# An attention and two-MoE kernel on one Trainium2 core: scores of a head pair in two PSUM groups instead of four, masks first, and the first weights' bit operations on every second slot

## The chip, the cores and the metric

The kernel runs on one core of one Trainium2 chip, which computes the whole output. The metric is the device time of the execution in microseconds; 3 runs of the kernel before are shown. A profiled execution of it gives the trace that is read here.

## What is computed

The reference, cut to what matters. Attention over 2 batches of 12 heads (448 positions, 64 wide), then two feed-forward stages on 896 tokens:

```python
scores = where(triu(ones, k=1), -1e9, q @ k.T / 8)      # causal, 24 heads of 448 x 448
p = exp(scores - max(scores)); attn = p / (sum(p) + 1e-9)
x = (attn @ v)                                          # -> 896 x 768
x = (sigmoid(x @ w_gate) * (x @ w_val)) @ w_out         # 768 -> 1536 -> 768
h = x @ w_in                                            # 768 -> 1024
out = (layernorm(h * softmax(h)) * g_ln) @ w_out2       # 1024 -> 768
```

All is held as a high and a low part (`hi`, `lo = value - hi`), and a product is three matmuls: hi·hi, hi·lo, lo·hi.

## The kernel before

The 24 heads are worked as 12 pairs p = 0 to 11. A head has four row blocks i = 0 to 3 of 128 query rows (block 0 has 64 new rows); block i sees keys 0 to QE[i], that is 64, 192, 320, 448 columns. For every block and both heads of a pair: the score matmuls (L333, `s`, six of 64 rows, two heads at a time on the two halves of the array), the mask added by a matmul with an identity (L336), the row maximum on VectorE (DVE, L354), exp with its row sum on ScalarE (ACT, L360, an ACTIVATE and a read of its accumulator for each head). Then sums (L366, GpSimd = POOL), reciprocals (L371, DVE), normalising of the probabilities `p` in place (L379, POOL), transposes on TensorE (PE, L404, `t`, four units a pair: (unit 1, head 0), (1, 1), (0, 0), (0, 1)), their split into hi (`tr_hi`, ACT L411) and lo (`tr_lo`, DVE L225 `pt`), and the product with v (L434, `x`, eight chunks a pair), split by `x_hi` (ACT L218 `xy`) and `x_lo` (DVE L225 `xy`). The splits of k and q for the next pair stand in the same loop: `k_hi` on ACT, `k_lo` on DVE (L225 `qks`), `q_hi` on POOL, `q_lo` on DVE (L245); those of v on POOL (`v_hi` L220, `v_lo` L225).

Nothing is scheduled by a tool: the loop `for s in range(slots + 34)` issues instructions by hand, and every engine works through its own list in the order in which it was issued. A pair has 8 slots. `SIDE`, `UNIT0` and `PV0` say in which slot, counted from the pair's own first, a step is issued; within a slot PE's work comes first, then ACT's, DVE's, POOL's. Waits between engines are put in by the framework from what a tile reads and writes. Two instructions of different engines on the same PSUM bank of one tile are always made to wait for each other, two readers included.

Scores have the pool `ps_s`: two buffers of `[128, 2, 512]` floats, one PSUM bank for each head of the pair. Before, each row block has a buffer of its own, so a pair goes through four, at slots 0, 2, 4, 6, in the order of `ORD` (blocks 3, 2, 1, 0).

From slot 74 on (pair 9's third slot) the loop also carries the bit operations that turn the first weight chunks, read from HBM as 64-bit words, into float32 (`bits_steps`: L112 on ACT, then L115, L117, L120 on DVE, then `dma_next` issues the load of a later chunk on SP), and the split of a chunk (`chunk_hi` ACT L131, `chunk_lo` DVE L134). From slot 96 on PE has `early_tiles`: 36 matmuls (L467, `gv`) of the first gate and value tile for batch 0, two a slot. After the loop follow the gate and value matmuls (L592), 383 us up to the end.

Of the kernel before, what the change touches and what calls it, by code (L numbers as in the profile page):

```python
# [10 lines left out]
F32 = mybir.dt.float32  # L11
# [24 lines left out]
NEG = -1e30  # L36
TERMS = ((0, 0), (0, 1), (1, 0))
# [7 lines left out]
def attn_moe_moe2(ctx: ExitStack, tc: tile.TileContext, qk, v, w_gv, w_out, w_in2, w_out2, g_ln, out):  # L45
# [3 lines left out]
    nc = tc.nc  # L49
# [11 lines left out]
    identb = const.tile([128, 128], BF16, name="identb")  # L61
    maskb = const.tile([128, 128], BF16, name="maskb")
# [111 lines left out]
    NE = 1  # L174
# [15 lines left out]
    with ExitStack() as actx:  # L190
# [4 lines left out]
        st = actx.enter_context(tc.tile_pool(name="st", bufs=2, side="right"))  # L195
        ps_s = actx.enter_context(tc.tile_pool(name="ps_s", bufs=2, space=PSUM, reuse_waits="tile"))
# [3 lines left out]
        NH = B * H  # L200
# [88 lines left out]
        NPB = 6  # L289
# [21 lines left out]

        rs_t, pt_t, ps_sc, ps_tr, ps_pv = {}, {}, {}, {}, {}

        def slot(s):

            return s // 8 * 2 + s % 2, ORD[s % 8 // 2]


        def sc_mm(s):
            if s % 2:  # L320
                return
            both = ps_s.tile([128, 2, 512], F32, tag="s", name="s")
# [17 lines left out]
        def sums_of(s):  # L340
            h, i = slot(s)
            t = sum_t[h // 2 % 3]
            k = NQ * (1 - h % 2) + i
            return t[:, k:k + 1], t[:, 8 + k:9 + k]

        def sc_max(s):
            if s % 2:
                return
            if s == 0:
                for e in range(2):  # L350
                    nc.vector.reduce_max(out=sums_of(e)[1], in_=ps_sc[e], axis=AX.X, negate=True)
                return
            h, i = slot(s)
            nc.vector.reduce_max(out=sum_t[h // 2 % 3][:, 8 + i:16:NQ], in_=ps_sc.pop((s, 2)), axis=AX.X, negate=True)  # L354

        def sc_exp(s):
            h, i = slot(s)
            n = QE[i]
            sm, mx = sums_of(s)
            nc.scalar.activation(out=p_t[h % NPB][:, POFF[i]:POFF[i] + n], in_=ps_sc.pop(s), func=AF.Exp,  # L360
                                 bias=mx, scale=1.0, accum_out=sm)


        def sums(p, u):
            rs = rs_t[p, u] = st.tile([128, 8], F32, tag=f"rs{u}", name="rs")
            nc.gpsimd.tensor_scalar(out=rs[:, 4:8].rearrange("p (a i) -> p a i", a=2),  # L366
                                    in0=sum_t[p % 3][:, 0:8].rearrange("p (a i) -> p a i", a=2)[:, :, 2 - 2 * u:4 - 2 * u],
                                    scalar1=EPS_SUM, scalar2=0.0, op0=ALU.add, op1=ALU.add)

        def recips(p, u):  # L370
            nc.vector.reciprocal(out=rs_t[p, u][:, 0:4], in_=rs_t[p, u][:, 4:8])  # L371

        def normalise(p, u):
            r = rs_t.pop((p, u))
            for i in (3 - 2 * u, 2 - 2 * u):
# [45 lines left out]
        def pv_mm(pr):  # L421
            ps = ps_pv[pr] = ps_x.tile([128, S], F32, tag="x", name="x")
            terms = {(a, j): iter(TERMS) for a in range(2) for j in range(NQ)}
            n = 0
            for chunk in CHUNKS:
                for w in chunk.split():
                    sec, j = int(w[0]), int(w[1])
                    h = 2 * pr + sec
                    u = 1 if j in UNITS[1] else 0
                    c0 = {0: 0, 1: 0, 2: 320, 3: S}[j]  # L430
                    a, c = next(terms[sec, j])

                    l = v3[pr % 2][:, a] if j == 3 else v2[pr % 2][:, a, j, (1 - sec) * D:(3 - sec) * D]
                    nc.tensor.matmul(out=ps[:, 128 * j:], lhsT=l, rhs=pt_t[h][:, c, u, c0:c0 + S - 128 * j],  # L434
                                     start=(n == 0), stop=(n == 20),
                                     skip_group_check=True)
                    n += 1
                yield
# [16 lines left out]
        def early_tiles():  # L455
# [23 lines left out]
        UNIT0 = {(1, 0): 11, (1, 1): 13, (0, 0): 15, (0, 1): 17}
        PV0 = 15  # L480

        SIDE = dict(
            kh=-6, qh=-6, kl=-4, ql=-3, sm0=5, rc0=6, nm0=6, lk=7, sm1=9, rc1=10, nm1=10, vh=12, vl=13, xh=23, xl=24)
        STEP = dict(
            qh=(prep_q_hi, 'P'), kh=(prep_k_hi, 'A'), kl=(prep_k_lo, 'D'), ql=(prep_q_lo, 'D'),
            vh=(prep_v_hi, 'P'), vl=(prep_v_lo, 'P'), lk=(last_keys, 'P'), xh=(x_hi, 'A'), xl=(x_lo, 'D'),
        )
        for u in range(2):
            STEP[f"sm{u}"] = (lambda p, u=u: sums(p, u)), 'P'
            STEP[f"rc{u}"] = (lambda p, u=u: recips(p, u)), 'D'  # L490
            STEP[f"nm{u}"] = (lambda p, u=u: normalise(p, u)), 'P'

        def side(s, eng):
            for name, s0 in SIDE.items():
                p, e = divmod(s - s0, 8)
                first = 1 if name[0] in "qk" else 0
                if STEP[name][1] == eng and e == 0 and first <= p < NH // 2:
                    STEP[name][0](p)
# [12 lines left out]
        for s in range(slots + 34):

            if (s - PV0) % 8 == 0 and 0 <= (s - PV0) // 8 < NH // 2:
                pv_now = pv_mm((s - PV0) // 8)
            at(sc_mm, s)
            if s in (2, 4, 6):
                keep_warm(24 if s == 2 else 8)
            for _ in range(2):  # L520
# [3 lines left out]
            next(pv_now, None)

            if s % 2 == 0:
                at(sc_exp, s - 2)
                at(sc_exp, s - 1)
            units(tr_hi, s - 1)
            side(s, 'A')  # L530

            side(s, 'D')
            units(tr_lo, s - 2)
            at(sc_max, s)

            side(s, 'P')
            side(s, 'S')
# [243 lines left out]
```

## Time and profile before

| | us |
|---|---|
| median of 3 runs (516.86 to 518.14) | 517.78 |
| the profiled execution | 517.47 |
| its span, from the first to the last instruction | 515.6 |
| PE busy / DVE / ACT / POOL | 501.2 (97%) / 335.7 / 227.0 / 141.9 |
| granted TensorE clock, mean | 0.992 |
| HBM traffic | 101 GB/s over the span |

Times in the rows below are microseconds from the span's start, "mean ns of one" apart. In a timeline a row is: start, duration, engine, line, operation, output <- inputs, shape, count, and in brackets the idle time of the engine just before it and what ended it. Matmuls overlap: a row of PE reaches into the next one. The granted clock is a share of 2.4 GHz: 1.00 is the full level, 0.50 the lower one, 1.2 GHz.

### The profile page before, as it was taken

The numbers are of one execution on the slowest core, as the hardware profiler recorded it, in microseconds if no ns is written. First come the engines' busy times: TensorE is split into PE (matmuls) and PEld (weight loads), VectorE is DVE, ScalarE is ACT, GpSimd is POOL, SyncE is SP. The second block draws the span as 40 slices with busy tenths as digits, with TensorE's granted clock in tenths as the row PEclk, the third lists the DMA queues.
The fourth block names the chain that finished last, engine by engine and source line by source line (L and its number), as shares of the span: only waits on it lengthen the run. The fifth ranks groups of instructions, "written<-read, shape, count | busy, mean of one in ns | idle before, by whom it ended". The sixth has DMA issues, their size and how long they took to land.

```text
span 515.6 us, 7727 instructions
## 1 busy us (share of the span) xinstructions
PE 501.2 (97%) x2900; PEld 448.9 (87%) x2900; DVE 335.7 (65%) x532; ACT 227.0 (44%) x481; POOL 141.9 (28%) x275
## 2 busy tenths in 40 slices
PE   8799999888999999999999999999999999999997
PEld 7588887778899999999999999999998888899997
DVE  6688878896356678877777766666763878741210
ACT  5677878673424443454345432432323243332211
POOL 2998888683000000000000000000051487720000
PEclk9999999799999999999999999999999999999999
DMA  5723232221122354444334531443450231000101
GB/s 149 214 67 105 64 107 58 82 83 62 62 89 96 103 161 128 160 163 141 122 112 158 184 107 59 163 163 123 163 182 2 72 114 62 0 32 31 62 32 61
DMA packets 13205, 52.80 MB, mean 102 GB/s; under 512 B 1776, under 2 KB 2288, under 8 KB 13168
## 3 DMA queue, kind: packets, MB, share of 16 engines
q1 hardware_dynamic: 13168, 52.31, 30.7%
q8 instruction: 23, 0.38, 0.3%
q14 instruction: 14, 0.11, 0.1%
HBM read 49.55 MB, written 2.75 MB: 101 GB/s over the span
## 4 chain that ended last, share of the span: by engine, by line
PE 90%; POOL 5%; DVE 2%; ACT 1%; issue 1%; POOLq 0%; ACTq 0%
PE gv L592 33%; PE pm L622 17%; PE po L713 11%; PE h L652 11%; PE x L434 5%; PE s L333 4%; PE t L404 4%; POOL p L379 3%; PE s L336 1%; PE gv L467 1%; PE tp L695 1%; PE warm L304 1%; ACT p L360 1%; POOL v L225 1%; POOL rs L366 0%
## 5 line engine op out<-in xcount | busy, mean ns | idle before, releaser
L592 PE MATMUL gv<-xy,hl 128*128 128x448 f32 x828 | 168.1, 365 | 0.6 <-ACT pre L472 0.6
L592 PEld LDWEIGHTS gv<-xy,hl 128*128 128x128 f32 x828 | 155.4, 188 | 13.3 <-ACT pre L472 1.0
L622 PE MATMUL pm<-g,hl 128*128 128x448 f32 x432 | 87.7, 365 | 0.0
L622 PEld LDWEIGHTS pm<-g,hl 128*128 128x128 f32 x432 | 81.1, 188 | 6.4
L639 POOL TENSOR_SCALAR t<-t,g_sb 128x768 f32<-128x768 f32 x8 | 9.0, 1121 | 257.9 <-PE pm L622 257.9
L134 DVE TENSOR_TENSOR hl<-t,hl 128x768 fp32r<-128x768 f32 x36 | 34.6, 962 | 40.9 <-ACT hl L131 39.2
L713 PE MATMUL po<-wo,lt 128*128 128x384 f32 x336 | 60.7, 340 | 0.0
L652 PE MATMUL h<-wi,xy 128*128 128x512 f32 x252 | 59.2, 395 | 0.0
L434 PE MATMUL x<-pt,v 128*128 128x320 f32 (+3 forms) x252 | 59.2, 336 | 0.0
L713 PEld LDWEIGHTS po<-wo,lt 128*128 128x128 f32 x336 | 58.7, 188 | 0.2 <-POOL wo L644 0.2
L652 PEld LDWEIGHTS h<-wi,xy 128*128 128x128 f32 x252 | 47.2, 187 | 11.4
L360 ACT ACTIVATE p<-s,sum 128x448 f32<-128x448 f32 (+3 forms) x96 | 44.9, 476 | 25.0 <-DVE sum L354 18.6
L117 DVE SCALAR_TENSOR_TENSOR t<-raw,t 128x768 int32<-128x768 int32 (+1 forms) x56 | 53.7, 958 | 1.8
L112 ACT ACTIVATE raw<-raw 128x768 f32<-128x768 f32 (+1 forms) x56 | 48.2, 868 | 12.2 <-DMA raw<-in_wo_dram 7.9
L120 DVE SCALAR_TENSOR_TENSOR t<-raw,t 128x768 int32<-128x768 int32 (+1 forms) x56 | 51.1, 913 | 1.6
L379 POOL TENSOR_SCALAR p<-p,rs 128x448 f32<-128x448 f32 (+3 forms) x96 | 47.1, 509 | 7.2 <-DVE rs L371 6.7
L354 DVE TENSOR_REDUCE sum<-s 128x2 f32<-128x640 f32 (+3 forms) x47 | 31.8, 677 | 15.5 <-PE s L336 15.3
L434 PEld LDWEIGHTS x<-pt,v 128*128 128x128 f32 x252 | 40.0, 195 | 0.4
L225 DVE TENSOR_TENSOR pt<-t,pt 128x512 fp32r<-128x512 f32 (+1 forms) x48 | 32.1, 668 | 5.1 <-ACT pt L411 4.8
L115 DVE TENSOR_SCALAR t<-raw 128x768 int32<-128x768 int32 (+1 forms) x56 | 30.7, 548 | 5.3 <-ACT raw L112 5.2
L333 PE MATMUL s<-qks 64*128 64x448 f32 (+3 forms) x288 | 32.9, 334 | 0.7 <-ACT p L360 0.7
L171 DVE TENSOR_TENSOR lt<-tp,lt 128x512 fp32r<-128x512 f32 x14 | 9.7, 690 | 36.4 <-ACT lt L170 36.4
(84 smaller groups left out, 518.7 us busy)
## 6 DMA issues: line engine op xcount, KB each, us to landing
raw<-in_gv_dram SPq DMA_DIRECT2D x24, 768.0 KB, 4.4
raw<-in_wo_dram SPq DMA_DIRECT2D x20, 768.0 KB, 4.4
raw<-in_wi_dram SPq DMA_DIRECT2D x12, 512.0 KB, 3.5
qkr<-in_qk_dram SPq DMA_DIRECT2D x22, 224.0 KB, 3.7
vr<-in_v_dram SPq DMA_DIRECT2D x12, 256.0 KB, 3.7
out_dram<-o SPq DMA_DIRECT2D x6, 384.0 KB, 2.3
qkr<-in_qk_dram SPq DMA_DIRECT2D x4, 112.0 KB, 2.7
out_dram<-o SPq DMA_DIRECT2D x2, 192.0 KB, 1.9
```

What stands on the lines that cost most here:

```text
L112: nc.scalar.activation(out=w1.bitcast(F32), in_=w1.bitcast(F32), func=AF.Copy, scale=2.0 ** -112)
L117: nc.vector.scalar_tensor_tensor(out=tt, in0=w1, scalar=-2 ** 31, in1=tt, op0=ALU.bitwise_and, op1=ALU.bitwise_or)
L120: nc.vector.scalar_tensor_tensor(out=tt, in0=w0, scalar=29, in1=tt, op0=ALU.logical_shift_right, op1=ALU.bitwise_or)
L225: (nc.gpsimd if eng == 'P' else nc.vector).tensor_tensor(out=out, in0=a, in1=b, op=ALU.subtract)
L333: nc.tensor.matmul(out=ps[e], lhsT=flat[rows, cq * S + n - 128:cq * S + n], rhs=t[rows, ck, :n], start=(m == 0), stop=False)
L360: nc.scalar.activation(out=p_t[h % NPB][:, POFF[i]:POFF[i] + n], in_=ps_sc.pop(s), func=AF.Exp, bias=mx, scale=1.0, accum_out=sm)
L379: nc.gpsimd.tensor_scalar(out=t, in0=t, scalar1=r[:, k:k + 1], scalar2=1.0, op0=ALU.mult, op1=ALU.mult)
L434: nc.tensor.matmul(out=ps[:, 128 * j:], lhsT=l, rhs=pt_t[h][:, c, u, c0:c0 + S - 128 * j], start=(n == 0), stop=(n == 20), skip_group_chec ...
L592: nc.tensor.matmul(out=ps[i, b], lhsT=w[:, a, cs], rhs=xy[kk][:, x, b * S:(b + 1) * S], start=(kk == 0 and a == 0 and x == 0), stop=(kk == ...
L622: nc.tensor.matmul(out=ps[b], lhsT=w[:, a, cs], rhs=g_t[kk][:, x, b * S:(b + 1) * S], start=(kk == 0 and a == 0 and x == 0), stop=(kk == N ...
L652: nc.tensor.matmul(out=h[:, n * 512:(n + 1) * 512], lhsT=xy[kk][:, a, tk], rhs=wi[n * NK + kk][:, c], start=(kk == 0 and i == 0), stop=(kk ...
L713: nc.tensor.matmul(out=ps[n], lhsT=lts[k // 4][:, a, k % 4], rhs=wo[k][:, c, cs], start=(k == 0 and i == 0), stop=(k == NF2 - 1 and i == 2))
```

## The change

1. **Two groups a pair.** `GROUPS = [(3, 0), (2, 1)]`: blocks 3 and 0 share one bank per head (448 + 64 = 512 columns), and blocks 2 and 1 (320 + 192 = 512). A pair takes two buffers of `ps_s`, at slots 0 and 4. Within a group the four masks come first (the first of each bank opens it), then the twelve score matmuls.
2. **The steps of a pair** stand in one list `STEPS`: maxima at slots 0, 1, 4, 5, exps at 1, 2, 5, 6; the sums move from POOL to DVE, ahead of the reciprocals (slots 3 and 7); normalising at slots 4 (blocks 3, 0) and 8 (blocks 2, 1) on POOL, where before it was at 6 (blocks 3, 2) and 10 (blocks 1, 0). For pair 0 the second head is normalised on DVE. Splits of k, q and v move by one to three slots, `x_lo` from 24 to 23. Transposes and v products keep their slots.
3. **The first weights' bit operations** start at slot 88 in place of 74, a step every second slot, nine slots a chunk in place of ten.
4. `keep_warm` (matmuls without use at the start) three times 24, at slots 2, 5, 9, in place of 24, 8, 8 at 2, 4, 6.

```diff
+GROUPS = [(3, 0), (2, 1)]
-ORD = [3, 2, 1, 0]
...
-        def sc_mm(s):
-            if s % 2:
-                return
+        def sc_mm(p, g):
             both = ps_s.tile([128, 2, 512], F32, tag="s", name="s")
...
+            for i in GROUPS[g]:
+                n = QE[i]
+                w = min(n, 128)
+                ps = ps_sc[p, i] = both[:, :, c0:c0 + n]
+                for e in range(2):
+                    nc.tensor.matmul(out=ps[:, e, n - w:], lhsT=identb, rhs=maskb[:, 128 - w:],
+                                     start=(c0 == 0), stop=False, skip_group_check=True)
+                c0 += n
+            for i in GROUPS[g]:
+                n = QE[i]
+                for m, (cq, ck) in enumerate(((1, 0), (1, 3), (2, 0))):
...
-        def sums(p, u):
-            rs = rs_t[p, u] = st.tile([128, 8], F32, tag=f"rs{u}", name="rs")
-            nc.gpsimd.tensor_scalar(out=rs[:, 4:8].rearrange("p (a i) -> p a i", a=2),
...
+        def recips(p, g):
+            rs = rs_t[p, g] = st.tile([128, 8], F32, tag=f"rs{g}", name="rs")
+            i = slice(0, 4, 3) if g == 0 else slice(1, 3)
+            nc.vector.tensor_scalar(out=rs[:, 4:8].rearrange("p (a i) -> p a i", a=2),
+                                    in0=sum_t[p % 3][:, 0:8].rearrange("p (a i) -> p a i", a=2)[:, :, i],
+                                    scalar1=EPS_SUM, scalar2=None, op0=ALU.add)
+            nc.vector.reciprocal(out=rs[:, 0:4], in_=rs[:, 4:8])
...
+                    eng = nc.vector if p == 0 and a else nc.gpsimd
...
+            (1, 'A', lambda p: sc_exp(p, 3)), (2, 'A', lambda p: sc_exp(p, 0)),
+            (5, 'A', lambda p: sc_exp(p, 2)), (6, 'A', lambda p: sc_exp(p, 1)),
+            (0, 'D', lambda p: sc_max(p, 3)), (1, 'D', lambda p: sc_max(p, 0)),
+            (4, 'D', lambda p: sc_max(p, 2)), (5, 'D', lambda p: sc_max(p, 1)),
...
-            if s in (2, 4, 6):
-                keep_warm(24 if s == 2 else 8)
+            if s in (2, 5, 9):
+                keep_warm(24)
...
-                e = s - 74 - 10 * c
+                e = s - 88 - 9 * c
                 if e == 0:
                     bits_now = bits_steps(c)
-                if 0 <= e < 4:
+                if e in (0, 2, 4, 6):
                     next(bits_now)
-                if e == 5 and c < 2 * NE:
+                if e == 7 and c < 2 * NE:
                     chunk_hi(c)
-                if e == 6 and c < 2 * NE:
+                if e == 8 and c < 2 * NE:
                     chunk_lo(c)
```

Three places show what moved. First, DVE in a middle pair, from one pair's widest maximum on, with the semaphores that an instruction waits for (`Activation_49` is counted up by ACT, `PE_49` by PE). Before (L354 the maxima, L371 the reciprocals):

```order
L354 TENSOR_REDUCE sum_141<-s 128x2 [waits PE_49]
L225 TENSOR_TENSOR pt<-t,pt 128x448 [waits Activation_49]
L371 RECIPROCAL rs<-rs 128x4 [waits Pool_49]
L354 TENSOR_REDUCE sum_141<-s 128x2 [waits PE_49]
L225 TENSOR_TENSOR pt<-t,pt 128x512 [waits Activation_49]
L225 TENSOR_TENSOR qks<-qkr,qks 128x448 [waits DMAHW4_49,DMAHW5_49,DVE_49,Activation_49]
L354 TENSOR_REDUCE sum_141<-s 128x2 [waits PE_49]
L245 SCALAR_TENSOR_TENSOR qks<-qkr,qks 128x448 [waits Pool_49]
L225 TENSOR_TENSOR pt<-t,pt 128x512 [waits DVE_49,Activation_49]
L371 RECIPROCAL rs<-rs 128x4 [waits Pool_49]
L354 TENSOR_REDUCE sum_141<-s 128x2 [waits PE_49]
```

After (L347 the maxima, L361 the sums, L364 the reciprocals), from the widest maximum to the fourth and what follows it:

```order
L347 TENSOR_REDUCE sum_139<-s 128x2 [waits PE_49]
L225 TENSOR_TENSOR pt<-t,pt 128x448 [waits Activation_49]
L347 TENSOR_REDUCE sum_139<-s 128x2 [waits Activation_49]
L225 TENSOR_TENSOR qks<-qkr,qks 128x448 [waits DMAHW1_49,DMAHW0_49]
L225 TENSOR_TENSOR pt<-t,pt 128x512 [waits Activation_49]
L361 TENSOR_SCALAR rs<-sum_139 128x4 [waits Activation_49]
L364 RECIPROCAL rs<-rs 128x4 [waits DVE_49]
L347 TENSOR_REDUCE sum_139<-s 128x2 [waits PE_49]
L225 TENSOR_TENSOR pt<-t,pt 128x512 [waits Activation_49]
L347 TENSOR_REDUCE sum_139<-s 128x2 [waits Activation_49]
L245 SCALAR_TENSOR_TENSOR qks<-qkr,qks 128x448 [waits Pool_49]
L225 TENSOR_TENSOR pt<-t,pt 128x512 [waits Activation_49]
```

Before, each of the four maxima waits for PE alone; now the first of a group waits for PE and the second for ACT, which has just read the other columns of the same bank.

Second, PE in a middle pair. Before, the two smaller blocks (L333 scores, L336 masks, L404 transposes, L434 v products):

```order
L333 MATMUL s<-qks 128x192 x6
L336 LDWEIGHTS identb
L336 MATMUL s<-maskb,identb 128x128
L336 LDWEIGHTS identb
L336 MATMUL s<-maskb,identb 128x128
L434 MATMUL x<-pt,v_1_136 128x448
L404 MATMUL t<-identx,p_145 128x128
L404 MATMUL t<-ident,p_145 128x128 x4
L434 MATMUL x<-pt,v_1_136 128x448 x2
L333 MATMUL s<-qks 128x64 x6
```

After, the second group of a pair (L334 scores, L325 masks, L429 v products):

```order
L325 LDWEIGHTS identb
L325 MATMUL s<-maskb,identb 128x128
L325 LDWEIGHTS identb
L325 MATMUL s<-maskb,identb 128x128
L325 LDWEIGHTS identb
L325 MATMUL s<-maskb,identb 128x128
L325 LDWEIGHTS identb
L325 MATMUL s<-maskb,identb 128x128
L334 MATMUL s<-qks 128x320 x6
L334 MATMUL s<-qks 128x192 x6
L429 MATMUL x<-pt,v_1_136 128x448
```

The six matmuls of a small block now follow those of a large one with no transposes or v products between.

Third, DVE where the first weight chunk's bit operations begin. Before, in pair 9, three slots in a row:

```order
L354 TENSOR_REDUCE sum_139<-s 128x2
L225 TENSOR_TENSOR pt<-t,pt 128x512
L115 TENSOR_SCALAR t<-raw 128x768
L225 TENSOR_TENSOR qks<-qkr,qks 128x448
L354 TENSOR_REDUCE sum_139<-s 128x2
L117 SCALAR_TENSOR_TENSOR t<-raw,t 128x768
L245 SCALAR_TENSOR_TENSOR qks<-qkr,qks 128x448
L225 TENSOR_TENSOR pt<-t,pt 128x512
L120 SCALAR_TENSOR_TENSOR t<-raw,t 128x768
```

After, in pair 11, which has no k and q of a next pair to split:

```order
L347 TENSOR_REDUCE sum_141<-s 128x2
L115 TENSOR_SCALAR t<-raw 128x768
L225 TENSOR_TENSOR pt<-t,pt 128x512
L361 TENSOR_SCALAR rs<-sum_141 128x4
L364 RECIPROCAL rs<-rs 128x4
L347 TENSOR_REDUCE sum_141<-s 128x2
L117 SCALAR_TENSOR_TENSOR t<-raw,t 128x768
L225 TENSOR_TENSOR pt<-t,pt 128x512
L347 TENSOR_REDUCE sum_141<-s 128x2
L120 SCALAR_TENSOR_TENSOR t<-raw,t 128x768
```

The three operations stand where the splits of k and q stood in the pairs before, or beside a maximum that waits.

## Rows read from the trace of the kernel before

**Rows 1.** Busy time by stretch: length, then each engine's, clock, DMA share, GB/s

```profile
30.31:81.57 51.26, 51.26 (x433) 41.70 (x432) 42.92 (x79) 40.28 (x134) 44.73 (x97) 1.00 0.32 85
81.57:132.53 50.96, 45.12 (x316) 37.95 (x315) 38.25 (x61) 30.15 (x85) 30.64 (x61) 0.93 0.25 81
132.53:515.60 383.07, 379.74 (x1904) 348.70 (x1904) 234.56 (x332) 137.22 (x203) 47.40 (x73) 1.00 0.30 103
```

**Rows 2.** Timeline of PE, pair 5: its widest block, and what follows

```profile
47.40 0.89 PE L333 MATMUL s<-qks 64*128 64x448 f32 x6
...
48.31 0.60 PE L434 MATMUL x<-pt,v 128*128 128x320 f32 x3
```

**Rows 3.** Timeline of PE around the bit operations: starts of pairs 9 and 11, waits

```profile
81.57 0.89 PE L333 MATMUL s<-qks 64*128 64x448 f32 x6
...
91.75 0.45 PE L404 MATMUL t<-identx,p 128*128 128x128 f32 x1 [2.43 <-DVE pt L225]
...
104.26 0.88 PE L333 MATMUL s<-qks 64*128 64x448 f32 x6
...
118.73 0.33 PE L404 MATMUL t<-identx,p 128*128 128x128 f32 x1 [1.12 <-POOL p L379]
...
132.53 0.69 PE L592 MATMUL gv<-xy,hl 128*128 128x448 f32 x2 [0.62 <-ACT pre L472]
```

**Rows 4.** Timelines of DVE and POOL there, and the stretch of lower clock

```profile
88.50 1.71 DVE L117 SCALAR_TENSOR_TENSOR t<-raw,t 128x768 int32<-128x768 int32 x1
...
91.52 0.94 DVE L120 SCALAR_TENSOR_TENSOR t<-raw,t 128x768 int32<-128x768 int32 x1
...
88.39 2.12 POOL L225 TENSOR_TENSOR v<-vr,v 128x384 fp32r<-128x384 f32 x2
...
91.70:97.80 6.10, 6.05 (x28) 5.05 (x28) 4.65 (x9) 3.16 (x11) 3.30 (x7) 0.50 0.48 167
```

**Rows 5.** Timeline of DVE, pair 5

```profile
48.54 1.09 DVE L354 TENSOR_REDUCE sum<-s 128x2 f32<-128x896 f32 x1 [0.72 <-PE s L336]
...
50.73 0.83 DVE L354 TENSOR_REDUCE sum<-s 128x2 f32<-128x640 f32 x1 [0.48 <-PE s L336]
...
52.18 0.79 DVE L225 TENSOR_TENSOR qks<-qkr,qks 128x448 fp32r<-128x448 f32 x1
52.89 0.55 DVE L354 TENSOR_REDUCE sum<-s 128x2 f32<-128x384 f32 x1
53.36 0.61 DVE L245 SCALAR_TENSOR_TENSOR qks<-qkr,qks 128x448 fp32r<-128x448 f32 x1
53.89 0.68 DVE L225 TENSOR_TENSOR pt<-t,pt 128x512 fp32r<-128x512 f32 x1
...
54.64 0.29 DVE L354 TENSOR_REDUCE sum<-s 128x2 f32<-128x128 f32 x1
...
55.75 0.62 DVE L225 TENSOR_TENSOR xy<-x,xy 128x448 fp32r<-128x448 f32 x1
```

**Rows 6.** Timeline of ACT, pair 5: first and last instruction of two blocks' exps

```profile
49.73 0.64 ACT L360 ACTIVATE p<-s,sum 128x448 f32<-128x448 f32 x1 [1.54 <-DVE sum L354]
...
50.87 0.20 ACT L360 ACTIVATION_READ_ACCUMULATOR p<-s,sum 128x1 f32 x1
...
51.90 0.54 ACT L360 ACTIVATE p<-s,sum 128x320 f32<-128x320 f32 x1
...
52.82 0.22 ACT L360 ACTIVATION_READ_ACCUMULATOR p<-s,sum 128x1 f32 x1
```

**Rows 7.** Timeline of DVE: widest maxima of pairs 0 and 2, last reciprocals of pair 11

```profile
7.88 1.16 DVE L351 TENSOR_REDUCE sum<-s 128x1 f32<-128x448 f32 x2 [1.44 <-PE s L336]
...
22.47 1.09 DVE L354 TENSOR_REDUCE sum<-s 128x2 f32<-128x896 f32 x1 [1.21 <-PE s L336]
...
117.98 0.17 DVE L371 RECIPROCAL rs<-rs 128x4 f32<-128x4 f32 x1
```

**Rows 8.** Costliest groups, the page's section 5: normalising on POOL

```profile
L379 POOL TENSOR_SCALAR p<-p,rs 128x448 f32<-128x448 f32 (+3 forms) x96 | 47.1, 509 | 7.2 <-DVE rs L371 6.7
```

More of the change, by code (lines that the diff above doesn't have):

```diff
@@ L340, in sums_of @@
[L340 to L354, printed above, removed]
@@ L370, in recips @@
[L370 to L375, printed above, removed]
+        def sc_mm(p, g):
+            both = ps_s.tile([128, 2, 512], F32, tag="s", name="s")
+            t = qk_sp[p]
+            flat = t.rearrange("p c s -> p (c s)")
+            c0 = 0
+            for i in GROUPS[g]:
[9 more added lines that the diff above has]
+                for m, (cq, ck) in enumerate(((1, 0), (1, 3), (2, 0))):
+                    for e in range(2):
+                        rows = slice(e * D, (e + 1) * D)
+                        nc.tensor.matmul(out=ps_sc[p, i][:, 1 - e], lhsT=flat[rows, cq * S + n - 128:cq * S + n],
+                                         rhs=t[rows, ck, :n], start=False, stop=(m == 2), skip_group_check=True)
@@ L419, in attn_moe_moe2, with pv_mm @@
         CHUNKS = ('01 01 02', '01 02 02', '11 11 12', '11 12 12', '00 00', '00', '10 10', '10 13 13 13')
[L421 to L438, printed above, removed]
+        pv_terms = {}
+        def pv_mm(pr, chunk):
+            if chunk == 0:
+                ps_pv[pr] = ps_x.tile([128, S], F32, tag="x", name="x")
+                pv_terms.update({(a, j): iter(TERMS) for a in range(2) for j in range(NQ)})
+            ps = ps_pv[pr]
+            words = CHUNKS[chunk].split()
+            for n, w in enumerate(words):
+                sec, j = int(w[0]), int(w[1])
+                h = 2 * pr + sec
+                u = 1 if j in UNITS[1] else 0
+                c0 = {0: 0, 1: 0, 2: 320, 3: S}[j]
+                a, c = next(pv_terms[sec, j])
+                l = v3[pr % 2][:, a] if j == 3 else v2[pr % 2][:, a, j, (1 - sec) * D:(3 - sec) * D]
+                nc.tensor.matmul(out=ps[:, 128 * j:], lhsT=l, rhs=pt_t[h][:, c, u, c0:c0 + S - 128 * j],
+                                 start=(chunk == 0 and n == 0), stop=(chunk == 7 and n == len(words) - 1),
+                                 skip_group_check=True)
         def x_parts(pr):
@@ L473, in early_tiles @@
                     yield True
-        slots = NH * NQ
+        NPR = NH // 2
+        PER = 8
         early = early_tiles()
         left = NE * 6 * NK
[L479 to L486, printed above, removed]
-        )
@@ L488, in attn_moe_moe2 @@
[L488 to L498, printed above, removed]
@@ L520, in attn_moe_moe2, with steps @@
+        def steps(s, eng):
+            for s0, e, f in STEPS:
+                p, r = divmod(s - s0, PER)
+                if e == eng and r == 0 and (1 if s0 < 0 else 0) <= p < NPR:
+                    f(p)
+        for s in range(PER * NPR + 27):
+            if s in (2, 5, 9):
+                keep_warm(24)
+            steps(s, 'E')
             for _ in range(2):
-                if s >= slots and left and next(early):
+                if s >= PER * NPR and left and next(early):
                     left -= 1
-            units(tr_mm, s)
@@ L524, in attn_moe_moe2 @@
[L524 to L537, printed above, removed]
+            steps(s, 'A')
+            steps(s, 'D')
+            steps(s, 'P')
             if s in (8, 12):
```

70 lines of the change are left out of this document (31 added, 39 removed).

## The prediction

> **What bounds the kernel now.** I read the busy times by stretch first. From 132.53 us on nothing differs but the moment at which the gate matmuls begin: 383.07 us, PE busy in 379.74 [rows 1]. The change touches what lies before. From 30.31 to 81.57 us, six pairs, PE is busy all the time, and a pair takes 51.26 / 6 = 8.54 us [rows 1]. DVE is busy in 42.92 of these 51.26 us, 7.15 a pair, POOL in 44.73. So PE bounds the middle, and the others have about 1.1 to 1.4 us a pair to spare. What idle time DVE has there lies ahead of a maximum that waits for PE, 0.72 and 0.48 us [rows 5].
>
> Next I read PE's timeline where the bit operations start. Pairs 9 and 10 take 104.26 - 81.57 = 22.69 us where two middle pairs take 17.08, so 5.6 are lost [rows 3]. PE waits 2.43 us for a lo split on DVE, behind L117, which took 1.71 us; the granted clock then stands at 0.50 from 91.70 to 97.80 [rows 3, 4]. Later PE waits 1.12 us for normalising on POOL, and the gate matmuls start at 132.53 [rows 3].
>
> **The change, step by step.**
>
> *PE.* The widest block with its masks lasts 48.31 - 47.40 = 0.91 us [rows 2]. Its columns are 3 x 448 scores, two heads at once, and 2 x 128 mask columns: 1600 columns at 2.4 GHz are 0.67 us. The rest, 0.24, is entry and exit, paid by each of four groups now and by two after. PE's work falls by 0.48 to some 8.06 us a pair. That is worth something only if PE still bounds the pair.
>
> *The new wait.* The order after shows the second maximum of each group waiting for ACT. DVE must finish the wide maximum, ACT must do both heads' exps, and only then may DVE read the few columns beside them. No row of before shows such a wait, but all its pieces have rows. From the widest maximum to its partner: 1.09 for the maximum, 0.10 to ACT (48.54 + 1.09 = 49.63 to 49.73), exps and accumulators 50.87 + 0.20 - 49.73 = 1.34, and 0.05 back (estimate, half of 0.10): 2.58 us [rows 5, 6]. DVE has one lo split of 0.53 to do meanwhile. For the second group: 0.83 + 0.10 + (52.82 + 0.22 - 51.90 = 1.14) + 0.05 = 2.12 [rows 5, 6], one lo split of 0.60 inside. Queued behind each waiting maximum stand a k or q split, a lo split, the sums and the reciprocals, and for these POOL's normalising waits, and then PE's transposes.
>
> The Trainium skill (PSUM — Partial Sum Buffer, Terms) says that two engines on one bank and the same partitions at once are an error, two readers included. No run here shows that error; the order shows the wait that avoids it, and the sum above needs only the order.
>
> *One round of DVE.* From the first maximum of a pair to that of the next, with starts a little before the end of the instruction ahead, as the rows show:
> - maximum of block 3 to that of block 0: 2.58;
> - block 0's maximum 0.21 (0.29 less the usual overlap of 0.08), k_lo 0.71 (52.18 to 52.89), lo split 0.60 (0.68 less 0.08), sums and reciprocals 0.28: 1.80 [rows 5];
> - maximum of block 2 to that of block 1: 2.12;
> - block 1's maximum 0.47, q_lo 0.53, lo split 0.60, sums and reciprocals 0.28, x_lo 0.54 with 0.14 of waiting for its hi: 2.56 [rows 5].
>
> Together 9.06 us. The sums on DVE have no row; between 0.05 and 0.4 I take 0.17, like a reciprocal of the same four columns [rows 7], with 0.03 for the wait between the two. That DVE's list is the round and not PE's follows from the same numbers: 9.06 against 8.06. POOL needs less than before, as two sums leave it. Transposes of the pair come back in time: behind the reciprocals POOL needs 1.6 us for three of the four operations at a mean of 0.509 [rows 8], PE some 2.3 (two eighths of its 8.06 and a little) for transposes, v products and the second group, while DVE comes to that group's maximum only 4.9 us after the reciprocals. So pairs in the middle go from 8.54 to about **9.05 us**, 0.5 slower, though PE has less to do.
>
> *The start.* The widest maximum of pair 0 now waits for its whole group, six more matmul pairs: 7.88 + 0.43 = 8.3 [rows 7]. Two rounds of 8.1 and 8.0 follow (9.06 less x_lo and lo splits that have nothing yet to split; the normalising of pair 0 on DVE falls into the waits). Pair 2 begins at 24.4, against 22.47 [rows 7]: 1.9 later. PE also stands idle about 2.3 us in the middle of pair 1's first group, until q_lo of that pair, which now stands behind the fourth maximum of pair 0. A gap of 2.43 us was followed by the lower clock [rows 3, 4]. PE is not the bound at the start, so I charge 0.5 us for that, between 0 and 2.5 (a little less than half of 6.10 us at half clock).
>
> *The middle and the bits.* Nine rounds lead to pair 11's widest maximum: 24.4 + 9 x 9.05 = 105.9. Its own round carries L115, L117, L120. L115 stands in k_lo's place, L117 mostly in the wait for ACT, L120 (0.94 [rows 4]) in q_lo's place: together some 0.2 us more. x_lo's 0.68 lies behind the reciprocals, so these are done 9.06 + 0.2 - 0.68 = 8.6 us after the maximum, at 114.5; before, at 117.98 + 0.17 = 118.15 [rows 7]. That is the gain: the stall of 5.6 us is gone, though 0.5 us a pair and 1.9 at the start were paid for it.
>
> *The tail.* The first transposes that need these reciprocals come 2.2 us behind them (three POOL operations, and two early matmuls ahead of them that wait for the first chunk's lo part): 116.7, against 118.73 [rows 3]. From there PE needed 132.53 - 118.73 = 13.8 us [rows 3]; four more of the 36 early matmuls lie behind this point now, 0.8 us. The gate matmuls begin at 131.3. Bits of chunks 2 and 3 end some 3 us into them, before PE needs them 7 us in. The loads of later chunks, on SP behind each chunk's last step, are issued up to 17 slots later, still nine or more slots, some 10 us, ahead of their use.
>
> *Sum.* 131.3 + 0.5 (clock) - 132.53 = -0.7 us. Against the profiled execution 517.47 - 0.7 = 516.8; the median of the runs stands 0.3 higher, so 517.1, and I predict **517.0 us**.
>
> **The rivals.**
>
> *PE stays the bound.* If the alternation of DVE and ACT costs less than the rows say, the round falls to PE's 8.06 to 8.4 us; for that POOL and ACT leave room [rows 1]. It would take 0.7 us off DVE's round, more than all sums and hand-overs together; the waits themselves are in the order. With 8.3: 9 x -0.75 = -6.8, and 510.3 us.
>
> *Slower: DVE and POOL hold each other up.* L117 took 1.71 us while POOL's v_lo ran from 88.39, and L120 of the same size 0.94 beside nothing [rows 4]. Now k_lo stands about 3.4 us behind the reciprocals, and POOL reaches v_lo about 3.5 behind them (four normalising operations are 2.0 [rows 8]; q_hi and the two of v_hi, of the same kind, another 1.5 by the same mean). If POOL comes first in most pairs, k_lo pays up to 0.7 in each, in DVE's round, where before q_lo started just ahead of v_lo and kept its 0.61 [rows 5]. With 0.5 in each of nine rounds the time is 517.0 + 4.5 = 521.5 us. It decides from about 0.25 us a pair on, 519.3.
>
> The Trainium skill (GPSIMD Engine Reference, Specifications) says that GpSimd's way into SBUF is shared with VectorE and that instructions of VectorE with two SBUF inputs contend for it. The row of L117 agrees. By that rule k_lo and q_lo can be hit, the maxima and lo splits, which read PSUM, cannot.
>
> *The stall comes back.* Spread over slots, L117 and L120 could still delay lo splits of pair 11, and the clock falls there again: the 22.69 us stretch lost 5.6 for two chunks; one chunk in one pair would lose up to 2.5, and 519.5. Against it: L117 lies in a wait now.
>
> **How the numbers follow.** The bound of what can be told from no change is 0.3%, 1.55 us: faster is below 516.2, slower above 519.3. My forecast, a round of 8.9 to 9.2 us, covers 515.2 to 519.2 (nine rounds at +-0.15 are +-1.4, the clock at the start 0 to 2.5): chance 0.62, of which 0.22 is below 516.2 and 0.40 within the bound. PE as the bound, or a round below 8.9: 0.14, faster. Contention 0.16 and the returning stall 0.08: slower. Faster 0.36, same 0.40, slower 0.24. The range leaves out a tenth on each side: 511.5 to 521.0.
>
> **What would show it.** Right: in the middle PE idles about 1 us a pair, ahead of transposes, for lo splits or normalising; DVE's second maxima (L347) wait for exps (L354) about 1.0 and 0.8 us; a pair takes 9.05 us; no stretch of 0.50 clock between 80 and 110 us; gate matmuls start near 131. Wrong: a pair at 8.1 to 8.4 with PE busy throughout (first rival); k_lo at 1.2 us or more beside v_lo (second); a gap of over 2 us ahead of transposes beyond 100 us (third).

## The result, and the profile after

The changed kernel takes 521.34 us (520.61 to 521.59), the kernel before 517.96 beside it: ratio 1.0067, 95% interval 1.0049 to 1.0085. It is slower by 3.4 us, where 517.0 was predicted with a range up to 521.0. The time lies at the price that the prediction gave to its second rival, contention between DVE and POOL (521.5); that this fits so closely is partly luck, as told below. Some executions of the kernel before, timed beside the runs below, took 519 to 521 us, at a mean granted clock of 0.987 to 0.989 where the others had 0.990 to 0.997; its medians there count them in.

Busy time by stretch, after, with the columns of [rows 1]: the start, six middle pairs, the last pairs, and all from the gate matmuls on:

```profile
0.00:25.02 25.02, 20.20 (x226) 18.48 (x227) 16.44 (x58) 13.69 (x45) 9.54 (x26) 0.93 0.55 164
34.38:91.58 57.20, 50.99 (x435) 43.47 (x434) 47.93 (x91) 40.38 (x133) 41.81 (x85) 1.00 0.27 77
91.58:136.63 45.05, 40.00 (x297) 34.72 (x295) 36.59 (x63) 28.46 (x80) 27.05 (x50) 1.00 0.17 57
136.63:519.60 382.97, 379.72 (x1904) 348.76 (x1904) 237.00 (x335) 137.88 (x204) 47.39 (x73) 1.00 0.32 107
```

The last row answers to the last of [rows 1]: 382.97 against 383.07 us. All of the loss lies before the gate matmuls. Six middle pairs take 57.20 us, **9.53 a pair**, where they took 8.54, and PE, busy without a gap before, is idle in 6.2 of the 57.20.

PE after, where it waits in one middle pair, then the first transposes that need the last reciprocals of pair 11, then the first gate matmuls (these answer to [rows 3]):

```profile
64.74 0.30 PE L397 MATMUL t<-identx,p 128*128 128x128 f32 x1 [0.54 <-DVE pt L225]
...
67.97 0.30 PE L397 MATMUL t<-identx,p 128*128 128x128 f32 x1 [0.49 <-DVE rs L361]
...
122.04 0.33 PE L397 MATMUL t<-identx,p 128*128 128x128 f32 x1
...
136.63 8.58 PE L561 MATMUL gv<-xy,hl 128*128 128x448 f32 x41 [0.62 <-ACT pre L465]
```

PE waits for DVE twice a pair, 1.03 us together, and the gate matmuls start 4.1 us later than at 132.53.

DVE after, one round from the widest maximum to the next (L347 maxima, L361 sums, L364 reciprocals; it answers to [rows 5]):

```profile
62.98 1.08 DVE L347 TENSOR_REDUCE sum<-s 128x2 f32<-128x896 f32 x1
63.98 0.61 DVE L225 TENSOR_TENSOR pt<-t,pt 128x448 fp32r<-128x448 f32 x1
65.47 0.29 DVE L347 TENSOR_REDUCE sum<-s 128x2 f32<-128x128 f32 x1 [0.88 <-ACT p L354]
65.68 1.54 DVE L225 TENSOR_TENSOR qks<-qkr,qks 128x448 fp32r<-128x448 f32 x1
67.14 0.68 DVE L225 TENSOR_TENSOR pt<-t,pt 128x512 fp32r<-128x512 f32 x1
67.75 0.15 DVE L361 TENSOR_SCALAR rs<-sum 128x4 f32<-128x4 f32 x1
67.93 0.18 DVE L364 RECIPROCAL rs<-rs 128x4 f32<-128x4 f32 x1
68.03 0.79 DVE L347 TENSOR_REDUCE sum<-s 128x2 f32<-128x640 f32 x1
68.74 0.68 DVE L225 TENSOR_TENSOR pt<-t,pt 128x512 fp32r<-128x512 f32 x1
70.02 0.56 DVE L347 TENSOR_REDUCE sum<-s 128x2 f32<-128x384 f32 x1 [0.60 <-ACT p L354]
70.49 0.61 DVE L245 SCALAR_TENSOR_TENSOR qks<-qkr,qks 128x448 fp32r<-128x448 f32 x1
...
72.52 1.08 DVE L347 TENSOR_REDUCE sum<-s 128x2 f32<-128x896 f32 x1
```

The fourth row is `k_lo`: 1.54 us, where [rows 5] had 0.79 for the same instruction. POOL at that moment, `v_hi` and the larger of the two `v_lo`:

```profile
65.00 0.77 POOL L220 TENSOR_SCALAR v<-vr 128x384 fp32r<-128x384 f32 x2
65.73 1.01 POOL L225 TENSOR_TENSOR v<-vr,v 128x384 fp32r<-128x384 f32 x1
```

That it is so in most pairs, the durations of all twelve `k_lo` and `q_lo` after tell (ns, least, median and most, then the first and last start); in the rounds of pairs 3 to 10, eight in a row, `k_lo` takes 1.53 to 1.55 us:

```profile
L225 DVE TENSOR_TENSOR qks<-qkr,qks x12: 614/1536/1548, 4.6 to 103.8; 128x448 fp32r<-128x448 f32 x12
...
L245 DVE SCALAR_TENSOR_TENSOR qks<-qkr,qks x12: 614/615/624, 5.8 to 108.6; 128x448 fp32r<-128x448 f32 x12
```

So the theory to test: `v_lo` on POOL stretches `k_lo` by some 0.75 to 0.9 us in each round, DVE's list is the round, and the pairs pay it. Against it stood: the waits at the shared bank set the round and `k_lo` only fills them; `k_lo` is slow there for another reason; PE has not gained what the change is for.

### The profile page after: what moved, and what is told of

It is laid out like the page before. It is cut to its first block, busy times and chain, and to the rows that moved or that the text cites. A ratio compares the mean times of both kernels' runs of the same rounds, so it can differ in the third digit from the quotient of the medians.

```text
span 519.6 us, 7716 instructions
## 1 busy us (share of the span) xinstructions
PE 499.8 (96%) x2932; PEld 453.3 (87%) x2932; DVE 345.8 (67%) x560; ACT 227.3 (44%) x481; POOL 133.1 (26%) x247
## 4 chain that ended last, share of the span: by engine, by line
PE 78%; DVE 14%; ACT 5%; issue 1%; POOL 0%; POOLq 0%; ACTq 0%
PE gv L561 32%; PE pm L591 17%; PE po L682 11%; PE h L621 11%; DVE sum L347 5%; ACT p L354 5%; DVE pt L225 3%; DVE qks L225 3%; PE warm L304 2%; PE gv L460 1%; PE tp L664 1%; DVE qks L245 1%; DVE xy L225 1%; PE x L429 1%; DVE rs L364 1%
## 5 line engine op out<-in xcount | busy, mean ns | idle before, releaser
L354 ACT ACTIVATE p<-s,sum 128x448 f32<-128x448 f32 (+3 forms) x96 | 44.8, 473 | 32.9 <-DVE sum L347 29.5
L117 DVE SCALAR_TENSOR_TENSOR t<-raw,t 128x768 int32<-128x768 int32 (+1 forms) x56 | 52.8, 943 | 1.9
L429 PE MATMUL x<-pt,v 128*128 128x320 f32 (+3 forms) x252 | 53.6, 327 | 0.0
L373 POOL TENSOR_SCALAR p<-p,rs 128x448 f32<-128x448 f32 (+3 forms) x92 | 43.9, 496 | 31.6 <-DVE rs L364 29.1
L347 DVE TENSOR_REDUCE sum<-s 128x2 f32<-128x128 f32 (+3 forms) x47 | 31.7, 675 | 17.7 <-ACT p L354 17.5
L429 PEld LDWEIGHTS x<-pt,v 128*128 128x128 f32 x252 | 39.0, 189 | 2.2
L131 ACT CAST hl<-t 128x768 fp32r<-128x768 f32 x36 | 30.0, 833 | 4.8 <-PE pm L591 4.2
```

Source lines behind the costliest of these rows:

```text
L117: nc.vector.scalar_tensor_tensor(out=tt, in0=w1, scalar=-2 ** 31, in1=tt, op0=ALU.bitwise_and, op1=ALU.bitwise_or)
L347: nc.vector.reduce_max(out=sum_t[p % 3][:, 8 + i:16:NQ], in_=ps, axis=AX.X, negate=True)
L354: nc.scalar.activation(out=p_t[(2 * p + e) % NPB][:, POFF[i]:POFF[i] + n], in_=ps[:, 1 - e], func=AF.Exp, bias=mx, scale=1.0, accum_out=sm)
L373: eng.tensor_scalar(out=t, in0=t, scalar1=r[:, k:k + 1], scalar2=1.0, op0=ALU.mult, op1=ALU.mult)
```

## The experiments

Each was timed beside the kernel before on the same chip (medians of it 517.5 to 518.0).

**1. `v_lo` moved, DVE untouched.**

```diff
-            (9, 'P', prep_v_hi), (10, 'P', prep_v_lo),
+            (9, 'P', prep_v_hi), (13, 'P', prep_v_lo),
```

> The changed kernel with one number different: v_lo on POOL is issued three slots later, behind the normalising of the first group, where POOL sat idle; DVE's order is untouched. It then runs beside q_lo. Contention theory: k_lo falls to 0.6 to 0.8 us, q_lo (two inputs from SBUF as well) rises from 0.61 to 1.2 to 1.5, and the pair stays near 9.5 us, the time at 519 to 522. If q_lo is not touched, a pair of 8.8 us and 514. Rival (k_lo is slow at its place for a reason of its own, not for v_lo): k_lo stays at 1.5 us and the time at 521.

515.0 us, ratio 0.995 (0.994 to 0.997). DVE in a middle pair, then POOL's larger `v_lo` there:

```profile
63.02 0.29 DVE L347 TENSOR_REDUCE sum<-s 128x2 f32<-128x128 f32 x1 [0.88 <-ACT p L354]
63.22 0.63 DVE L225 TENSOR_TENSOR qks<-qkr,qks 128x448 fp32r<-128x448 f32 x1
...
66.67 0.56 DVE L347 TENSOR_REDUCE sum<-s 128x2 f32<-128x384 f32 x1 [0.60 <-ACT p L354]
67.15 0.61 DVE L245 SCALAR_TENSOR_TENSOR qks<-qkr,qks 128x448 fp32r<-128x448 f32 x1
```

```profile
67.17 1.47 POOL L225 TENSOR_TENSOR v<-vr,v 128x384 fp32r<-128x384 f32 x1
```

`k_lo` is at 0.63 and a pair at 8.78 us (52.70 us for six), 0.75 less, with both waits for ACT unchanged. That is the first half of the theory. The second half did not come: `q_lo`, now beside `v_lo`, keeps its 0.61, and it is `v_lo` that takes 1.47 in place of 1.01; so a pair and the time came out near the case written down for that, 8.8 and 514. Some 6 us of the change's time were this one meeting (521.3 against 515.0).

**2. `k_lo` and `q_lo` in each other's places.**

```diff
-            (-7, 'A', prep_k_hi), (-7, 'P', prep_q_hi), (-6, 'D', prep_k_lo), (-2, 'D', prep_q_lo),
+            (-7, 'A', prep_k_hi), (-7, 'P', prep_q_hi), (-2, 'D', prep_k_lo), (-6, 'D', prep_q_lo),
```

> The changed kernel with k_lo and q_lo in each other's places: the same inputs of SBUF, the same size, but q_lo (scalar_tensor_tensor) now starts where v_lo starts on POOL, and k_lo (tensor_tensor) beside normalising. If the contention is one of place and inputs: q_lo takes 1.3 to 1.6 us, the pair stays at 9.5 and the time at 520 to 522. If it depends on the operation, as the run with v_lo moved suggests (q_lo beside v_lo kept 0.61): q_lo stays at 0.6 to 0.8, the pair falls to 8.8 and the time to 514 to 516.

521.5 us, a pair 9.53. The twelve durations of `k_lo` and `q_lo`:

```profile
L225 DVE TENSOR_TENSOR qks<-qkr,qks x12: 615/616/624, 4.8 to 109.2; 128x448 fp32r<-128x448 f32 x12
```

```profile
L245 DVE SCALAR_TENSOR_TENSOR qks<-qkr,qks x12: 617/1540/1548, 5.8 to 104.3; 128x448 fp32r<-128x448 f32 x12
```

Place, not operation: `q_lo` inherits the 1.54 us.

**3. The larger `v_lo` in three pieces.**

```diff
-            sub('P', lo, r, f32(hi))
+            for j in range(3):
+                sub('P', lo[:, j], r[:, j], f32(hi[:, j]))
```

> The changed kernel with the larger of the two v_lo instructions on POOL cut in three of a third of its columns; nothing else moves. All traces so far fit one reading: POOL and DVE take turns by whole instructions, and a DVE split that starts while POOL is inside one waits for that one's end and then needs another 0.47 us. The large v_lo starts 0.05 us behind k_lo's start, is inside when k_lo asks, and ends 1.06 behind it: 1.06 + 0.47 = 1.53, and 1.54 is the row. Turns: with pieces of about 0.45 us (the small v_lo has 0.46 alone) k_lo takes 0.9 to 1.1 us, a pair falls by about 0.5 to 8.9 to 9.1, the time to 516 to 518. Rival (the two share throughput for as long as v_lo lasts, in whatever pieces): k_lo stays at 1.4 to 1.6 us and the time at 520 to 523, as POOL has more instructions.

514.2 us, a pair 8.71. `k_lo`, and POOL's first piece beside it:

```profile
61.93 0.61 DVE L225 TENSOR_TENSOR qks<-qkr,qks 128x448 fp32r<-128x448 f32 x1
```

```profile
61.99 0.88 POOL L225 TENSOR_TENSOR v<-vr,v 128x128 fp32r<-128x128 f32 x1
```

Shared throughput, as the rival has it, is out: POOL has more to do and `k_lo` pays nothing. The expectation by turns was wrong in who waits: here DVE goes first, and POOL's piece, 0.46 us elsewhere, takes 0.88; so a pair is shorter than the 8.9 to 9.1 expected. That one of the two waits until the other's instruction ends fits all three runs; what decides which, the runs do not show. In the changed kernel `k_lo` starts 0.05 us ahead of `v_lo` and loses, here 0.06 ahead and wins.

**4. `k_lo` moved on DVE.**

```diff
-            (-7, 'A', prep_k_hi), (-7, 'P', prep_q_hi), (-6, 'D', prep_k_lo), (-2, 'D', prep_q_lo),
+            (-7, 'A', prep_k_hi), (-7, 'P', prep_q_hi), (-3, 'D', prep_k_lo), (-2, 'D', prep_q_lo),
```

> The changed kernel with one number different: k_lo of the next pair is issued three slots later, between the lo split that follows the third maximum and the fourth maximum, where DVE sat idle 0.60 us for ACT. There POOL normalises and v_lo is over. Contention theory (v_lo on POOL stretches k_lo, 1.54 us in place of 0.64, in every round of DVE): k_lo back to 0.6 to 0.8 us, the stretch from the second maximum to the third falls from 2.56 to 1.1 to 1.4 us, a pair from 9.53 to 8.2 by DVE's list, or 8.3 to 8.5 if PE is then the bound; about 510 us, 508 to 513. Rival (the waits for ACT at the shared bank set the round by themselves and a shorter k_lo only lengthens another wait): k_lo short too, but a pair stays at 9.2 to 9.5 and the time at 518 to 521 us.

513.8 us, ratio 0.993 (0.991 to 0.995): just above the 508 to 513 expected, far below the rival. `k_lo` takes 0.71, a pair 8.66: 0.87 less, where 1.0 to 1.3 were expected. PE is idle once a pair now:

```profile
61.03 0.30 PE L397 MATMUL t<-identx,p 128*128 128x128 f32 x1 [0.54 <-DVE pt L225]
```

The lo split that ends this wait is queued behind the widest maximum. So what bounds the pair here is, as the rows read, a loop through two engines: from that split (start 60.27) over PE's transposes and second group to the third maximum (63.41), and from there over DVE's list, without a wait, to the next such split (68.93).

**5. Both maxima of a group ahead of the exps.**

```diff
-            (0, 'D', lambda p: sc_max(p, 3)), (1, 'D', lambda p: sc_max(p, 0)),
-            (4, 'D', lambda p: sc_max(p, 2)), (5, 'D', lambda p: sc_max(p, 1)),
+            (0, 'D', lambda p: sc_max(p, 3)), (0, 'D', lambda p: sc_max(p, 0)),
+            (4, 'D', lambda p: sc_max(p, 2)), (4, 'D', lambda p: sc_max(p, 1)),
```

> The changed kernel with both maxima of a group issued in one slot, ahead of the exps, so that neither waits for ACT at the shared bank. Idle time of DVE ahead of L347 of 0.88 and 0.60 us a pair should be gone. Contention theory: k_lo starts about 0.8 us earlier, ahead of most of v_lo, and shrinks to 0.7 to 1.0 us; a pair falls to 8.2 to 8.5, the time to 509 to 513 us. If the wait was the only cost and k_lo still meets v_lo at full length: a pair of 8.6 to 8.9, 513 to 516. Rival (PE has no less to do than before, its groups cost what they cost in four): a pair of 8.5 whatever DVE does, 511 to 513, with PE busy all through.

518.6 us, a pair 9.14: missed by all three. What DVE waited for in six pairs (us, times, longest), first the changed kernel, then this run:

```profile
DVE sum L347 <- ACT p L354: 8.9, 12, 0.9
```

```profile
DVE pt L225 <- ACT pt L404: 8.3, 12, 1.1
```

The wait at the bank is gone and the same wait stands one place on. The exps start later, behind two maxima; the hi part of the transposes stands behind the exps in ACT's list; and DVE's lo split needs that hi part. `k_lo` shrank to 0.73 here as expected. Beside run 1, where it took 0.63, a pair is 0.36 us longer (9.14 against 8.78), and `k_lo` accounts for only 0.10 of that. Taking the wait at the shared bank away gains nothing here: DVE waits about as long one step later, for a split that ACT does behind its exps.

**6. Both splits in the waits.**

```diff
-            (-7, 'A', prep_k_hi), (-7, 'P', prep_q_hi), (-6, 'D', prep_k_lo), (-2, 'D', prep_q_lo),
+            (-7, 'A', prep_k_hi), (-7, 'P', prep_q_hi), (-7, 'D', prep_k_lo), (-3, 'D', prep_q_lo),
```

> The changed kernel with two numbers different: both splits of the next pair's q and k lie in DVE's two waits for ACT: k_lo between the lo split behind the widest maximum and the second maximum (idle 0.88 us there), q_lo between the lo split behind the third maximum and the fourth (idle 0.60). There POOL normalises; v_lo comes later. Contention theory with the waits filled: DVE's list gives 2.49 + 1.65 + 2.0 + 1.98 = 8.1 us, PE about the same, a pair of 8.1 to 8.4, 506 to 511 us. Rival (the alternation of DVE and ACT sets the round, as the run with both maxima early showed with 9.14): a pair of 8.6 or more, 513 us or more.

512.5 us, ratio 0.989 (0.986 to 0.993), a pair 8.71: the rival's pair, half a microsecond below its time. Two meetings with POOL, and a new wait for ACT:

```profile
60.70 0.93 DVE L225 TENSOR_TENSOR qks<-qkr,qks 128x448 fp32r<-128x448 f32 x1
...
62.74 0.52 DVE L361 TENSOR_SCALAR rs<-sum 128x4 f32<-128x4 f32 x1
...
66.92 0.17 DVE L361 TENSOR_SCALAR rs<-sum 128x4 f32<-128x4 f32 x1 [0.37 <-ACT p L354]
```

`k_lo` meets `q_hi` and takes 0.3 us more, but within the wait: from the first maximum to the second 2.49 us pass, as in the changed kernel. The sums, 0.15 us alone, meet `v_lo`, and from the second maximum to the third 1.74 us pass, where 1.65 were expected. What is missing lies behind the fourth maximum: without `q_lo` 1.98 us were expected up to the next pair's widest maximum, and 2.51 came, as the sums of the second group now wait 0.37 for ACT's exps. So here it is ACT, more than POOL, that takes back what the moves gave.

**7. Without maxima from pair 3 on.** The exps take the maxima of three pairs before as their shift.

```diff
         def sc_max(p, i):
+            if p > 2:
+                return
```

> The changed kernel without its row maxima from pair 3 on (the exps use the maxima of three pairs before as their shift), so DVE has 2.7 us less a pair and neither wait at the shared bank. That shows what PE needs for a pair in two groups: 8.06 us by the prediction's sum, 8.0 to 8.3 with k_lo still beside v_lo but in a list with room; 507 to 511 us. Rival (two groups save PE nothing): 8.5 a pair with PE busy all through, 512 to 514.

506.1 us, a little below the 507 to 511 expected. Two pairs, from one group's masks to the same masks two pairs on:

```profile
57.13:72.96 15.83, 15.83 (x146) 14.46 (x145) 10.33 (x23) 13.42 (x45) 14.64 (x29) 1.00 0.33 91
```

PE is busy in all 15.83 us: 7.92 a pair, where four groups took 8.54. Two groups do save 0.62 us of PE a pair; how much of it is the entry and exit that the prediction charged, no run shows.

**8. and 9. The bit operations alone.** On the kernel before the new timing; on the changed kernel the old one:

```diff
-                e = s - 74 - 10 * c
+                e = s - 88 - 9 * c
...
-                if 0 <= e < 4:
+                if e in (0, 2, 4, 6):
...
```

> The kernel before with one part of the change alone: the first weights' bit operations start at slot 88, a step every second slot, nine slots a chunk. By the prediction the stall of 5.6 us in pairs 9 and 10 goes, with no 0.50 clock between 80 and 110 us, and at most 0.5 to 1 us of it comes back in pair 11: 512 to 514 us. Rival (the stall moves to pair 11 and behind it, with a clock drop there): 516 to 518 us.

512.6 us (510.9 to 515.1), ratio 0.991 (0.988 to 0.995). In the profiled execution, which took 515.1, the clock stood at 0.80, a mean of both levels, in the stretch from 5 to 26 us. From 80 to 110 us nothing is lost:

```profile
80.00:110.00 30.00, 30.00 (x258) 24.15 (x255) 25.47 (x46) 25.06 (x82) 26.16 (x57) 1.00 0.16 43
```

PE is busy throughout and the clock full, where [rows 3, 4] had a gap of 2.43 us and 6.10 us at 0.50.

> The changed kernel with the first weights' bit operations as before: from slot 74 on, four slots in a row, ten slots a chunk. Alone on the kernel before the later start was worth 4.9 us (517.5 to 512.6). If that value is the same here: 526 us, 524 to 528. If DVE as the bound of the pairs makes every bit operation in pairs 9 to 11 count in full (6 operations of 0.5 to 1.7 us, with POOL's splits beside them): 527 to 530. If the waits for ACT swallow them: 521 to 523.

526.8 us, as expected, and 5.4 above the changed kernel: the value of the later start is about 5 us in either kernel, and it adds up with the rest. So all the rest of the change, the two groups with their new order and `keep_warm`, costs some 8.7 us (521.3 against 512.6), and the bits gave 4.9 back. What `keep_warm` does by itself was not measured.

**10. and 11. `k_lo` and `x_lo` moved; then also without the sums.** `k_lo` stands as in run 4, and `x_lo` in the wait ahead of the second maximum. Run 11 leaves out the instruction L361 as well; its reciprocals read the row sums themselves.

```diff
-            (23, 'A', x_hi), (23, 'D', x_lo),
+            (23, 'A', x_hi), (25, 'D', x_lo),
```

> The changed kernel with k_lo behind the third maximum (as in the run that moved it alone, 8.66 us a pair) and x_lo moved two slots on, into DVE's wait of 0.88 us ahead of the second maximum. x_lo reads PSUM, and no row shows it stretched by POOL. In the run with k_lo moved alone the loop went from the third maximum over DVE's list (with x_lo in it) to the widest maximum and the lo split behind it, then over PE's transposes and second group back to the third maximum. Without x_lo's 0.54 in it: 8.1 to 8.2 a pair, 507 to 510 us. Rival (DVE and ACT set the round, whatever is moved into the waits, as the runs with 8.66 and 8.71 would have it): 8.6 to 8.7 a pair and 512 to 514 us.

511.3 us, ratio 0.986 (0.983 to 0.988), a pair 8.43: between the two expectations. `x_lo` is in the wait at its usual 0.61; of the 0.54 us 0.23 came, and the sums now stand beside `v_lo`:

```profile
62.19 0.80 DVE L361 TENSOR_SCALAR rs<-sum 128x4 f32<-128x4 f32 x1
```

```profile
61.95 1.01 POOL L225 TENSOR_TENSOR v<-vr,v 128x384 fp32r<-128x384 f32 x1
```

The first row is the sums on DVE, four columns in 0.80 us, in the loop; the second the `v_lo` on POOL that they meet.

> As the run with k_lo and x_lo moved, and the sums' instruction is left out: the reciprocal reads the sums themselves, without the 1e-9 (a sum is at least 1, so that float32 does not change). DVE has 0.2 us less in each group. If DVE's list is still in the loop: 7.9 to 8.0 a pair, PE as the bound (7.92 in the run without maxima), 1 to 2 us below the run with the sums, 506 to 508. If PE bounds already: no difference to it, within 1 us.

508.0 us, **ratio 0.980 (0.977 to 0.982)**: 10 us faster than the kernel before, 13 than the changed one. Some 5 of the 10 are the later bit operations (run 8). Six pairs:

```profile
40.07:88.77 48.70, 48.70 (x433) 43.23 (x434) 42.42 (x79) 40.45 (x134) 43.70 (x84) 1.00 0.33 90
```

8.12 a pair with PE busy in all of it: of the 0.62 us that two groups save on PE 0.42 arrive. The gain over run 10, 3.3 us, is more than the 1 to 2 expected for one short instruction. The reciprocals, which now stand beside the same `v_lo`, do not wait as the sums did:

```profile
59.92 0.17 DVE L361 RECIPROCAL rs<-sum 128x4 f32<-128x4 f32 x1
```

```profile
59.47 1.01 POOL L225 TENSOR_TENSOR v<-vr,v 128x384 fp32r<-128x384 f32 x1
```

## Why the prediction was wrong

**The step that failed is one term of DVE's round:** from block 0's maximum to that of block 2, 1.80 us, with 0.71 for `k_lo` taken from [rows 5]. It measured 2.56 (65.47 to 68.03), as `k_lo` took 1.54. The sum held nothing for DVE and POOL meeting there. The price for this was worked out, as a rival with 0.16: 0.5 us a pair, and 521.5. It was given too little for two reasons that could have been read. First, I let chance decide who comes first, "in most pairs", while the rounds of the middle are alike: in eight rounds in a row it was `k_lo` that waited. Second, [rows 4] had a meeting at its full size, L117 at 1.71 in place of 0.94, and of these 0.77 I charged 0.5. That the time then fell on the rival's 521.5 is partly luck: a meeting costs a pair 0.75, so 0.25 more than charged, and without it a pair takes 8.78 (run 1), 0.27 less than the sum's 9.05.

The parts, against the rows:

- PE's work, 8.06 a pair: 7.92 when nothing else bounds (run 7). Right in kind, a saving of 0.62 where 0.48 was charged.
- The waits for ACT, about 1.0 and 0.8: 0.88 and 0.60. The stretches from a group's first maximum to its second, 2.58 and 2.12: 2.49 and 1.99; from the fourth to the next pair's widest, 2.56: 2.50. All a little long. So by nine rounds the forecast of about 517 would have been too high by some 2 without the meeting (estimate, 9 x 0.27), and was too low by 4 with it.
- The start, pair 2's widest maximum at 24.4: 25.02. `k_lo` of pair 1, 1.28 us beside `v_lo`, is not what makes it late: in run 1 it takes 0.61, and pair 2 starts at 25.18. In both the third maximum of pair 1 waits for PE, here 0.20, in run 1 0.84:

```profile
21.09 0.82 DVE L347 TENSOR_REDUCE sum<-s 128x2 f32<-128x640 f32 x1 [0.20 <-PE s L334]
```

```profile
21.25 0.82 DVE L347 TENSOR_REDUCE sum<-s 128x2 f32<-128x640 f32 x1 [0.84 <-PE s L334]
```

The gap of 2.3 us on PE in pair 1's first group is there to the digit (2.30, for `q_lo`), and between 12.5 and 22.5 us the granted clock is 0.83, a mean of both levels, where it was 1.00 before. So "PE is not the bound at the start" was wrong, while the 0.5 charged for the clock was near.

- Nine rounds to pair 11's widest maximum: 85.65 us in place of 81.5, so 4.2 of the miss. The bits in that pair's round, and its reciprocals 8.98 after the maximum, not 8.6: 0.4.
- The tail: first dependent transposes 2.4 behind the reciprocals (2.2 predicted), the gate matmuls 14.6 behind these (13.8 + 0.8 = 14.6). Right. Together 0.6 + 4.2 + 0.4 + 0.2, less the 0.5 charged for the clock, which the measured start contains: 4.9, and the gate matmuls came 4.8 after the 131.8 of the sum.
- The stall of 5.6 us goes: right, worth 4.9 and 5.4 in runs 8 and 9. The third rival did not come: the clock is 1.00 in all of the stretch after 91.58, and PE's longest wait ahead of transposes beyond 100 us is 0.91, not over 2.
- The first rival, PE as the bound, fails by 1.03 us of idle PE a pair; of the versions with two groups PE is busy throughout only in runs 7 and 11.
- That DVE's list with its two waits is the round holds while `k_lo` takes 1.54. With that gone other loops are as long: through PE in run 4, through ACT's splits and exps in runs 5 and 6. An instruction moved into a wait shortens a pair only if it leaves the loop that bounds then. These loops are read from the rows of one pair each.

## What to carry over

When an order is rewritten, write down for each DVE instruction whose inputs all lie in SBUF which POOL instruction runs beside it in the new order: in a steady loop the meeting is the same in every round, and one pair of instructions cost more here (0.75 us a pair) than the change saved on PE (0.62). A wait that is seen on one engine is not yet a cost: take it away in thought and look for the next wait for the same releaser (run 5). And work taken off the bound engine comes out only when the other engines' loop is shorter than what is left; here that took two moved splits and one instruction less, which had stood beside `v_lo`.

## What the runs showed of the hardware

In these runs POOL and DVE do not slow each other in proportion; one waits until the other's instruction ends. Rows of the changed kernel: `v_lo` ends at 65.73 + 1.01 = 66.74, and `k_lo` 0.48 later; alone it takes 0.62. In run 10 `v_lo` ends at 61.95 + 1.01 = 62.96, and the sums at 62.99. In run 1 it is POOL that waits, 1.47 for 1.01. The maxima and the lo splits of the transposes, which read PSUM, kept their durations beside POOL: in the runs shown the widest maximum takes 1.08 or 1.09, a split 0.61 to 0.69.

The Trainium skill (SBUF — State Buffer, Terms) says just this: the pair of ports that the two share is taken exclusively and held for the whole instruction, and the loser blocks. The traces agree, with the numbers above. Read so, [rows 4] offered 0.77 as the size of the term, where 0.5 was charged; the prediction had gone by the Trainium skill's summary (GPSIMD Engine Reference, Specifications), which speaks of contention alone. Two things more are in the rows. The sums, with one input of four columns, wait as well (0.80 and 0.52 us for 0.15), while the reciprocals of the same four columns take 0.17 beside `v_lo` (run 11). And which of the two goes first can't be read from their starts in the profile (runs 1 and 3).
